# Attention and mixture of experts on one core: loads and splits of the values, and reads of the first slot lists, moved to other turns of the head loop

## The chip, the cores and the metric

The kernel runs on one core of a Trainium2 chip. The metric is device time in microseconds (us) of one execution. Before the change the median of three runs is 532.14 us (531.71 to 534.35).

The engines of the core run side by side, each working through its own instructions strictly in the order in which the program was written: PE (TensorE: matmuls and transposes), DVE (VectorE), ACT (ScalarE), POOL (GpSimd), and SP (SyncE), which here only issues DMA transfers. An instruction that waits holds up everything behind it on its own engine.

## The reference

Causal softmax attention over 4 batches and 12 heads, with 448 positions and 64 numbers a head, then a mixture of 8 experts with one expert per token:

```
scores = q @ k.T / sqrt(64), masked above the diagonal
attn   = softmax(scores);  x = (attn @ v), heads side by side: [1792, 768]
logits = x @ w_gate + modality_bias[modality_id];  e = argmax(logits)
out    = softmax(logits)[e] * (relu(x @ w1[e]) @ w2[e])
```

Everything is float32 in and out. The kernel keeps the accuracy by splitting operands into a high and a low part.

## The kernel before, in words

**The head loop.** `iteration(n)` is called for n = 0 to 47; below it is called turn n. The 48 heads go through it as a pipeline, and one turn does the stages of several heads: scores of head n (`st_scores`, PE line 277), the exponentials of head n-1 (`st_exp`, ACT line 294), the transposes and the split of head n-2 (`st_trans`, PE lines 307 and 309; `st_split`, ACT line 327 and DVE line 328), the product with the values of head n-3 (`st_pv`, PE lines 341 and 348, called PV below), and the sum of its two parts (`st_low`, ACT line 366; `st_out`, DVE line 372, a turn later). Four heads are a group (GH = 4), and three groups are a batch. Group g is heads 4g to 4g+3; its first PV stands in turn 4g+3.

**Combining.** From turn 7 on PE also multiplies one tile of a finished group with the gate weights (`st_comb`, line 401). A turn later it is normalised: tiles 0 and 2 on DVE, tiles 1 and 3 on POOL (lines 419 and 429), for which ACT first copies them out of PSUM (`st_move`, line 411). So in each odd turn POOL begins with a normalisation that needs ACT's copy of what PE did at the end of the turn before.

**Queries and keys.** For each pair of heads m, SP loads `raw` (`load_qk`, line 179). POOL splits it in the odd turn 2m-3 (`split_qk`: line 185, line 186, and two halves of `kz` on line 189). SP then copies parts of the result to the other half of the partitions by four SBUF to SBUF transfers (`stack_qk`, lines 197 and 198), in the even turn 2m-2. The scores of head 2m, in turn 2m, read them.

**Values.** There is a single buffer `vraw` for the values of one group. SP loads it (`load_v`, lines 245 and 246); POOL writes the high part (`split_vh`, line 252) and the low part (`split_vl`, line 257) into `vhl`, of which there are two. The first PV of the group reads both parts. Before the change the values of group g are loaded at the end of turn 4g-2, the high part is made in turn 4g, late, and the low part in turn 4g+1, behind that turn's `split_qk`.

**The list of extra work.** `later(n, f)` puts f into turn n, ahead of `split_qk` and the splits of the values; `before` and `soon` put it at other points of a turn. On POOL these are: setting up constants in turns 4 and 6 to 11 (`shift_slots`, line 553 and 565), scatters of routed tokens into the tables (`scatter`, line 512) in turns 26, 28, 30 and 32 for the first batch and two each in turns 38 and 39 for the second, gathers of tokens (`fetch_x`, line 749), and splits of expert weights in turns 45, 46 and 47 (`w1_chunk`, lines 684 and 685). On SP: the slot lists of the first expert block (`pre_ids`, line 737, four small transfers each, which read the tables) and loads of the first expert's weights (`start_w1`, line 676). The constant n in `after_batch` is 31 for the second batch, to which the numbers 8, 11 and the list W1AT are added. After turn 47 a tail finishes the last heads, and the expert stage follows.

In turn n the order on POOL is: normalisation, list of turn n, `split_qk` (odd n), the group's sums (`st_sums`, turn 4g+1), the splits of the values.

Of the kernel before, what the change touches and what calls it, by code (L numbers as in the profile page):

```python
# [21 lines left out]
def attention_moe(  # L22
# [15 lines left out]
    B, HP, _, _, S = qk.shape  # L38
# [7 lines left out]
    GH = 4  # L46
    NG = H // GH
    NHEAD = B * H
# [97 lines left out]
    def T(shape, dt, tag, bufs):  # L146
        return atp.tile(shape, dt, tag=tag, name=tag, bufs=bufs)
# [44 lines left out]
    def stack_qk(m):  # L192
        st, hl = spl[2 * m]
        u, d = slice(0, 64), slice(64, 128)
        src = hl.bitcast(F32)
        for a, r in enumerate((u, d)):
            nc.sync.dma_start(out=st[u, a].bitcast(F32), in_=src[r, 1:3])
            nc.sync.dma_start(out=st[d, a].bitcast(F32), in_=src[r, 0:3:2])
        for a in range(2):
            spl[2 * m + a] = (st[:, a, 0], st[:, a, 1], hl[:, 1], kz[m % 2][:, a])  # L200

    def clear_kz(j):
        P.memset(kz[j][0:64, 1].bitcast(F32), 0.0)
# [38 lines left out]
    def load_v(gr):  # L242
        b, u = divmod(gr, NG)
        c = slice(u * GH * D, (u + 1) * GH * D)
        nc.sync.dma_start(out=vraw[:, 0:3, :], in_=v[b, 0:384, c].rearrange("(t p) c -> p t c", p=128))
        nc.sync.dma_start(out=vraw[0:64, 3, :], in_=v[b, 384:448, c])
# [3 lines left out]
    def split_vh(gr):  # L250
        t = T([128, NTL, GH, 2, D], F32R, "vhl", 2)
        P.tensor_scalar(out=t[:, :, :, 0], in0=vsrc, scalar1=1.0, scalar2=0.0, op0=ALU.mult, op1=ALU.add)
        vhl[gr] = t
# [115 lines left out]
    def st_out(g):  # L369
        gr, h = divmod(g, GH)  # L370
        j, a = divmod(h, 2)
        V.tensor_tensor(  # L372
            out=ots(gr, j)[a * 64:a * 64 + 64], in0=ov.pop(g)[0:64, :S], in1=ol.pop(g), op=ALU.add
        )
# [10 lines left out]
    def st_rec(gr):  # L385
        V.reciprocal(out=rec[gr], in_=rec[gr])
# [20 lines left out]
    def st_move(gr, i):  # L407
        if i % 2:
            c = cxt[:, (i // 2) * 384:(i // 2) * 384 + GH * XW]
            n = QT[i][1]  # L410
            A.activation(out=c[:n], in_=cx[gr, i][1][:n, :GH * XW], func=AF.Copy)
            cx[gr, i] = P, c
# [21 lines left out]
    def st_norm(gr, i):  # L434
        norm_l(gr, i)
        norm_x(gr, i)

    def x_store(b, i):
        q0, n = QT[i]
        t0 = b * S + q0  # L440
        nc.sync.dma_start(out=xs[t0:t0 + n, :], in_=xrow.pop((b, i))[:n])
# [258 lines left out]
    def reg(apx, engines, lo, hi):  # L700
        return nc.values_load(apx, engines=engines, min_val=lo, max_val=hi, skip_runtime_bounds_check_because=WHY)
# [21 lines left out]
    def places_of(t):  # L723
        return (0, 1) if t < PZ else (t % 2,)

    def fetch_ids(t, off, blk=0):
        d = early.tile([128, NTL, 2, 2], I32, tag="idq", name="idq", bufs=3)
        for i in range(NTL):
            o = d[:, i, blk]
            if t == 0 or PZ <= t < SZ:  # L730
                src = tables[i][bass.ds(off, BLK), :]
            elif t < PZ:
                o = d[:, i]
                src = tables[i][bass.ds(off, 2 * BLK), :].rearrange("(b p) c -> p b c", p=BLK)
            else:
                src = tables[i][bass.ds(off, HB), :].rearrange("(o p) c -> o p c", o=1).to_broadcast([2, HB, 2])
            nc.sync.dma_start(out=o, in_=src)
        idq[t, blk] = d

    def fetch_x(t, rows=NT, blk=None):  # L740
        d = idq.pop((t, blk or 0))
        n = BLK if t < SZ else HB
        for b, u in enumerate(places_of(t)):
            if blk not in (None, b):
                continue
            g = idg[t % 3][b]
            V.tensor_reduce(out=g[:, 0:1], in_=d[:, :, b, 0], axis=AX, op=ALU.min)
            V.tensor_reduce(out=g[:, 1:2].bitcast(F32), in_=d[:, :, b, 1].bitcast(F32), axis=AX, op=ALU.max)
            P.indirect_dma_start(  # L749
                out=xg[u][:n], out_offset=None, in_=xs[0:rows, :],  # L750
                in_offset=bass.IndirectOffsetOnAxis(ap=g[:n, 0:1], axis=0),
                bounds_check=rows - 1, oob_is_err=False,
            )
# [140 lines left out]
    with tc.manual_schedule():  # L894
# [103 lines left out]
        def later(n, f):  # L998
            todo.setdefault(n, []).append(f)

        def before(n, f):
            todo.setdefault((n,), []).append(f)

        def soon(n, f):
            todo.setdefault(-n, []).append(f)

        def run_todo(n):
            for f in todo.pop(n, ()):
                f()

        e0 = []
        W1AT = (7, 9, 14, 14, 15, 15)

        def start_w1(k):
            if k == 0:
                e0.append(reg(sch0[0:1, 0:1], [ET.SP], 0, E - 1))
            load_w(raw1, w1, e0[0], [k])

        def pre_ids(t):
            fetch_ids(0, reg(sch0[0:1, 1 + t:2 + t], [ET.SP], 0, EMPTY), t)  # L1020

        def after_batch(b, n):
            st = route(b)
            if b == B - 1:
                return st
            choose, places, rank, scatter = st
            for j, f in enumerate(choose, 1):
                (later if j % 2 else before)(n + 1 + j // 2, f)
            last = b == B - 2
            soon(n + 4, places)  # L1030
            for j, f in enumerate(rank, 1):
                (later if j % 2 else before)(n + 5 + j // 2, f)
            for i in range(NTL):
                later(n + 7 + (2 * i, i // 2, 0)[b], lambda i=i: scatter([i]))
            if b == 1:
                later(n + 6, first_expert)
                before(n + 7, first_slot)
                for k in range(K1):
                    later(n + W1AT[k], lambda k=k: start_w1(k))
                for j, f in enumerate((first_shift, first_base, first_tri, first_order)):  # L1040
                    later(n + 9 + j, f)
                for t in range(NPRE):
                    later(n + 8 + t, lambda t=t: pre_ids(t))
                    later(n + 11 + 2 * t, lambda t=t: fetch_x(0, 2 * S, t))

        g1b = {}

# [28 lines left out]
        def iteration(n):  # L1076
            if n and n % 2 == 0 and n + 2 < NHEAD:
                stack_qk((n + 2) // 2)
            gr, i = divmod(n - 2 * GH, GH)
            comb = 0 <= gr < B * NG  # L1080
            if 0 <= n - 4 < NHEAD:
                st_out(n - 4)
            if comb:
                st_move(gr, i)
                st_norm(gr, i)
                b, u = divmod(gr, NG)
                if u == NG - 1:
                    later(n + 1, lambda i=i: x_store(b, i))
                    if i == NTL - 1:
                        after_batch(b, n)  # L1090
            run_todo((n,))
            if n in (2, 3):
                st_trans(n - 2)
            if n < NHEAD:
                st_scores(n)
            if n == 0:
                subs.extend(first_split(1))
            if n == 1:
                for f in subs:
                    f()  # L1100
            run_todo(n)
            if n in (1, 3):
                clear_kz(n // 2)
            if n % 2 == 1 and n + 3 < NHEAD:
                split_qk((n + 3) // 2)
            if n % GH == 1 and n > GH:
                st_sums(n // GH - 1, P)
            if n % GH == RECAT and n > GH:
                st_rec(n // GH - 1)
            if n % GH == 1 and n < NHEAD:  # L1110
                split_vl(n // GH)
            if 0 <= n - 1 < NHEAD:
                st_exp(n - 1)
            if n % GH == 0 and n < NHEAD:
                split_vh(n // GH)
            if 0 <= n - 2 < NHEAD:
                if n > 3:
                    st_trans(n - 2)
                run_todo(-n)
                st_split(n - 2)  # L1120
            if 0 <= n - 3 < NHEAD:
                st_pv(n - 3)
                st_low(n - 3)
            gr, i = divmod(n - 2 * GH + 1, GH)
            if 0 <= gr < B * NG:
                st_comb(gr, i)
            if n % 2 == 0 and n + 6 < NHEAD:
                load_qk((n + 6) // 2)
            if n % GH == 2 and n // GH + 1 < B * NG:
                load_v(n // GH + 1)  # L1130

        for n in range(NHEAD):
            iteration(n)
# [47 lines left out]
        n = NHEAD  # L1181
# [238 lines left out]
```

## Time and profile before

| | |
|---|---|
| median of three runs | 532.14 us |
| lowest, highest | 531.71, 534.35 us |
| the profiled execution | 530.7 us, span 529.0 us from the first to the last instruction |
| granted TensorE clock, mean over the span | 0.974 |
| busy share of the span | PE 92%, DVE 60%, POOL 55%, ACT 52% |

The head loop takes about the first 215 us of the span, the expert stage the rest. The profile gives start and duration of each instruction, and for each one before which its engine stood idle, how long and what ended the idle time. Where several waits end together, the one named is the last to come, which need not be the one that mattered. The granted clock is a share: 1.00 is 2.4 GHz, 0.50 is 1.2 GHz.

### The profile page before, as it was taken

The numbers are of one execution on the slowest core, as the hardware profiler recorded it, in microseconds if no ns is written. First come the engines' busy times: TensorE is split into PE (matmuls) and PEld (weight loads), VectorE is DVE, ScalarE is ACT, GpSimd is POOL, SyncE is SP. The second block draws the span as 40 slices with busy tenths as digits, with TensorE's granted clock in tenths as the row PEclk, the third lists the DMA queues.
The fourth block names the chain that finished last, engine by engine and source line by source line (L and its number), as shares of the span: only waits on it lengthen the run. The fifth ranks groups of instructions, "written<-read, shape, count | busy, mean of one in ns | idle before, by whom it ended". The sixth has DMA issues, their size and how long they took to land. (4 is left out here: it accounts for less than half of the span.)

```text
span 529.0 us, 10530 instructions
## 1 busy us (share of the span) xinstructions
PE 486.8 (92%) x3427; PEld 456.9 (86%) x3427; DVE 319.3 (60%) x882; ACT 273.9 (52%) x683; POOL 290.2 (55%) x303
## 2 busy tenths in 40 slices
PE   4598999999988979989899999999999999989981
PEld 4498899999988879878899999999999999978761
DVE  7988888999999979898521114552011120394690
ACT  4498899998878848734321124442111211552830
POOL 7799999889899788973220200742001001194581
PEclk9799999999999979999899999999999999999987
DMA  8687789977977389756369300973101001077100
GB/s 210 176 195 194 198 217 247 277 195 204 241 207 203 114 214 278 240 162 92 90 186 381 93 32 1 295 259 106 62 1 50 31 8 68 20 266 248 25 12 6
DMA packets 44138, 80.77 MB, mean 153 GB/s; under 512 B 15646, under 2 KB 27166, under 8 KB 44064
## 3 DMA queue, kind: packets, MB, share of 16 engines
q1 hardware_dynamic: 41024, 68.89, 46.9%
q0 software_dynamic: 3040, 11.03, 6.3%
q8 instruction: 29, 0.48, 0.4%
q14 instruction: 45, 0.37, 0.3%
HBM read 49.01 MB, written 11.89 MB: 115 GB/s over the span
## 5 line engine op out<-in xcount | busy, mean ns | idle before, releaser
L294 ACT ACTIVATE p<-p,nm 128x448 f32<-128x448 f32 x192 | 94.7, 497 | 9.6 <-DVE nm L284 9.6
L749 POOL DMA_INDIRECT xg<-xs,idg x18 | 20.3, 1128 | 137.2 <-DVEq L1330 73.2
L787 DVE SCALAR_TENSOR_TENSOR htl<-g,hth 128x256 fp32r<-128x256 f32 x40 | 16.8, 423 | 109.5 <-ACT hth L786 109.5
L309 PE MATMUL pt<-ident,p 128*128 128x128 f32 x336 | 70.7, 281 | 0.0
L770 PE MATMUL g<-xh,w1l 128*128 128x256 f32 x240 | 67.9, 283 | 0.0
L769 PE MATMUL g<-xl,w1h 128*128 128x256 f32 x240 | 67.9, 283 | 0.0
L768 PE MATMUL g<-xh,w1h 128*128 128x256 f32 x240 | 67.9, 283 | 0.0
L328 DVE TENSOR_TENSOR pl<-pt,ph 128x1024 fp32r<-128x1024 f32 x48 | 58.4, 1217 | 13.1 <-ACT ph L327 12.9
L327 ACT ACTIVATE ph<-pt 128x1024 fp32r<-128x1024 f32 x48 | 48.9, 1020 | 15.6 <-PE pt L309 15.4
L341 PE MATMUL ot<-ph,vhl 128*128 128x448 f32 x192 | 50.9, 306 | 4.8 <-DVE ut L372 2.3
L189 POOL TENSOR_TENSOR kz<-raw,hl 64x448 fp32r<-64x448 f32 x44 | 51.5, 1170 | 6.4 <-DMA table<-ent,si 4.0
L786 ACT ACTIVATE hth<-g 128x256 fp32r<-128x256 f32 x40 | 15.2, 382 | 65.6 <-PE g L770 64.8
L307 PE MATMUL pt<-ident,p 128*128 128x64 f32 x288 | 49.1, 253 | 0.0
L309 PEld LDWEIGHTS pt<-ident,p 128*128 128x128 f32 x336 | 47.8, 170 | 0.2 <-issue 0.2
L277 PE MATMUL sa<-st 128*128 128x448 f32 x96 | 32.6, 340 | 16.2 <-DVE st L229 6.6
L828 POOL DMA_INDIRECT out_dram<-row,idg x14 | 14.8, 1055 | 57.5 <-ACTq L1314 32.2
L769 PEld LDWEIGHTS g<-xl,w1h 128*128 128x128 f32 x240 | 46.1, 192 | 0.0
L770 PEld LDWEIGHTS g<-xh,w1l 128*128 128x128 f32 x240 | 46.1, 192 | 0.0
L768 PEld LDWEIGHTS g<-xh,w1h 128*128 128x128 f32 x240 | 46.1, 192 | 0.0
L307 PEld LDWEIGHTS pt<-ident,p 128*128 128x128 f32 x288 | 45.0, 197 | 0.4
L341 PEld LDWEIGHTS ot<-ph,vhl 128*128 128x128 f32 x192 | 34.1, 197 | 6.4 <-POOL vhl L257 3.2
L284 DVE CUSTOM_DVE_ANT_0 p<-sa,mask 128x448 f32<-128x448 f32 x96 | 36.2, 413 | 3.3 <-PE sa L277 2.8
(337 smaller groups left out, 1434.1 us busy)
## 6 DMA issues: line engine op xcount, KB each, us to landing
st<-hl SPq DMA_DIRECT2D x88, 224.0 KB
raw<-in_moe_w_dram SPq DMA_DIRECT2D x24, 512.0 KB
raw<-in_qk_dram SPq DMA_DIRECT2D x22, 448.0 KB
raw<-in_moe_w_dram SPq DMA_DIRECT2D x20, 384.0 KB
vraw<-in_v_dram SPq DMA_DIRECT2D x12, 384.0 KB
xs<-row SPq DMA_DIRECT2D x12, 384.0 KB
ut<-in_moe_w_dram SPq DMA_DIRECT2D x6, 384.0 KB
raw<-in_qk_dram SPq DMA_DIRECT2D x8, 224.0 KB
```

The source lines that it names most:

```text
L189: P.tensor_tensor(out=kz[m % 2][r, a], in0=x[r, 1], in1=hl[r, 2].bitcast(F32), op=ALU.subtract)
L277: nc.tensor.matmul(outs[i], lhsT=a[:, q0:q0 + n], rhs=z[:, :w], start=(last == 0), stop=(last == 1))
L284: V.tensor_tensor_reduce(out=z, in0=o, in1=m, scale=-scale, scalar=3.0e38, op0=ALU.add, op1=ALU.min, accum_out=nm[:n, i:i + 1],)
L294: A.activation(out=z, in_=z, func=AF.Exp, bias=nm[:n, i:i + 1], scale=-1.0, accum_out=sums[:n, b, i, h:h + 1],)
L307: nc.tensor.matmul(o, lhsT=a, rhs=ident[:, r0:r1], start=True, stop=True)
L309: nc.tensor.transpose(out=o, in_=a, identity=ident)
L327: A.activation(out=ph, in_=t, func=AF.Copy)
L328: V.tensor_tensor(out=pl, in0=t, in1=ph.bitcast(F32), op=ALU.subtract)
L341: nc.tensor.matmul(o[:, q0:S], lhsT=t[:rows, kt, h].rearrange("p a d -> p (a d)"), rhs=ph[:rows, c0:c1], start=(n == 0), stop=(n == 1),)
L768: nc.tensor.matmul(o, lhsT=ah, rhs=bh, start=first, stop=False)
L769: nc.tensor.matmul(o, lhsT=ah, rhs=bl, start=False, stop=False)
L770: nc.tensor.matmul(o, lhsT=al, rhs=bh, start=False, stop=last)
```

## The change

- The load of the values of group g moves from the end of turn 4g-2 to the top of turn 4g, behind the four stack transfers of that turn. (Group 0 is loaded ahead of the loop, as before.)
- Both splits of the values of group g move to turn 4g+2, one behind the other. Before, they stood in turns 4g and 4g+1.
- The two reads of slot lists move from turns 39 and 40 to turns 41 and 42, and the gathers that use them from turns 42 and 44 to turns 44 and 45.
- The load of the first slice of expert weights moves from turn 38 to turn 39.

```
-        W1AT = (7, 9, 14, 14, 15, 15)
+        W1AT = (8, 9, 14, 14, 15, 15)
...
-                    later(n + 8 + t, lambda t=t: pre_ids(t))
-                    later(n + 11 + 2 * t, lambda t=t: fetch_x(0, 2 * S, t))
+                    later(n + 10 + t, lambda t=t: pre_ids(t))
+                    later(n + 13 + t, lambda t=t: fetch_x(0, 2 * S, t))
...
                 stack_qk((n + 2) // 2)
+            if n and n % GH == 0 and n < NHEAD:
+                load_v(n // GH)
...
-            if n % GH == 1 and n < NHEAD:
+            if n % GH == 2 and n < NHEAD:
+                split_vh(n // GH)
                 split_vl(n // GH)
             if 0 <= n - 1 < NHEAD:
                 st_exp(n - 1)
-            if n % GH == 0 and n < NHEAD:
-                split_vh(n // GH)
...
-            if n % GH == 2 and n // GH + 1 < B * NG:
-                load_v(n // GH + 1)
```

## Rows read from the trace of the kernel before

**Rows 1.** The first part of the profile's page: busy time of each engine, its share of the span, and its instructions.

```profile
PE 486.8 (92%) x3427; PEld 456.9 (86%) x3427; DVE 319.3 (60%) x882; ACT 273.9 (52%) x683; POOL 290.2 (55%) x303
```

**Rows 2.** Waits in the stretch from 12 to 215 us, that is the head loop: who waited for whom, us in total, times, longest. PEld is PE's loading of weights.

```profile
PEld ot L341 <- POOL vhl L257: 3.2, 4, 1.9
PE sa L277 <- DMA st<-hl: 3.1, 1, 3.1
```

**Rows 3.** The timeline of SP in turns 39 and 40: start, duration, instruction. A merged row of several transfers lasts from the first to the last.

```profile
176.89 6.87 SPq L737 DMA_DIRECT2D idq<-table  x4
183.87 0.48 SPq L197 DMA_DIRECT2D st<-hl  x1
```

**Rows 4.** Stretches of the span, from the view by windows: from:to, length, busy time (and count of instructions) of PE, PEld, DVE, ACT and POOL, granted clock, DMA share, GB/s.

```profile
169.24:170.72 1.48, 0.00 (x2) 0.00 (x1) 1.48 (x4) 1.02 (x1) 1.40 (x2) 1.00 0.88 234
185.06:188.17 3.11, 0.00 (x1) 0.03 (x1) 1.78 (x4) 2.10 (x9) 3.03 (x5) 0.95 0.98 217
188.17:195.00 6.83, 6.83 (x34) 6.61 (x34) 5.02 (x13) 1.24 (x2) 6.16 (x6) 0.52 0.74 204
195.00:199.19 4.19, 4.19 (x36) 3.73 (x35) 4.01 (x14) 4.14 (x13) 3.40 (x6) 1.00 0.95 251
252.90:254.79 1.89, 0.00 (x0) 0.00 (x0) 1.28 (x6) 1.89 (x3) 0.33 (x1) 1.00 0.24 4
254.79:259.50 4.71, 4.71 (x18) 4.71 (x19) 4.04 (x10) 0.03 (x1) 1.90 (x2) 0.64 0.58 157
```

**Rows 5.** The timeline of POOL in turns 4 to 6 (group 1): start, duration, instruction.

```profile
33.06 1.06 POOL L252 TENSOR_SCALAR vhl<-vraw 128x1024 fp32r<-128x1024 f32 x1
39.00 2.35 POOL L257 TENSOR_TENSOR vhl<-vraw,vhl 128x1024 fp32r<-128x1024 f32 x1
41.32 0.46 POOL L553 TENSOR_SCALAR by_shift<-tcol 128x1 f32<-128x1 f32 x2
41.84 0.34 POOL L553 TENSOR_SCALAR by_shift<-by_shift 128x1 f32<-128x1 f32 x2
```

**Rows 6.** The timeline of PE: the first PV of groups 1 and 2, with PE's idle time before it.

```profile
41.40 0.56 PE L341 MATMUL ot<-ph,vhl 128*128 128x448 f32 x2 [1.67 <-POOL vhl L257]
58.08 0.56 PE L341 MATMUL ot<-ph,vhl 128*128 128x448 f32 x2 [0.64 <-POOL vhl L257]
```

**Rows 7.** The timeline of POOL in turns 24 to 31 (groups 6 and 7).

```profile
109.82 1.04 POOL L252 TENSOR_SCALAR vhl<-vraw 128x1024 fp32r<-128x1024 f32 x1
112.75 0.24 POOL L419 TENSOR_TENSOR ltp<-cxt,rec 128x32 f32<-128x32 f32 x1 [1.89 <-ACT cxt L411]
...
118.44 2.39 POOL L257 TENSOR_TENSOR vhl<-vraw,vhl 128x1024 fp32r<-128x1024 f32 x1
...
127.84 1.03 POOL L512 DMA_INDIRECT table<-ent,si  x1 [0.28 <-POOL kz L189]
128.95 1.04 POOL L252 TENSOR_SCALAR vhl<-vraw 128x1024 fp32r<-128x1024 f32 x1
...
134.59 1.17 POOL L189 TENSOR_TENSOR kz<-raw,hl 64x448 fp32r<-64x448 f32 x1 [0.54 <-DMA table<-ent,si]
...
136.13 2.39 POOL L257 TENSOR_TENSOR vhl<-vraw,vhl 128x1024 fp32r<-128x1024 f32 x1
138.66 1.01 POOL L512 DMA_INDIRECT table<-ent,si  x1
139.70 0.25 POOL L419 TENSOR_TENSOR ltp<-cxt,rec 128x32 f32<-128x32 f32 x1
```

**Rows 8.** The timeline of PE: the first PV of groups 7, 10 and 11.

```profile
138.57 0.56 PE L341 MATMUL ot<-ph,vhl 128*128 128x448 f32 x2
...
197.37 0.55 PE L341 MATMUL ot<-ph,vhl 128*128 128x448 f32 x2
...
214.09 0.54 PE L341 MATMUL ot<-ph,vhl 128*128 128x448 f32 x2
```

**Rows 9.** The timeline of POOL in turns 36 to 46 (groups 9 to 11).

```profile
162.07 1.04 POOL L252 TENSOR_SCALAR vhl<-vraw 128x1024 fp32r<-128x1024 f32 x1
163.66 0.24 POOL L419 TENSOR_TENSOR ltp<-cxt,rec 128x32 f32<-128x32 f32 x1 [0.54 <-DMA st<-hl]
...
191.26 2.36 POOL L257 TENSOR_TENSOR vhl<-vraw,vhl 128x1024 fp32r<-128x1024 f32 x1
...
195.85 0.23 POOL L419 TENSOR_TENSOR ltp<-cxt,rec 128x32 f32<-128x32 f32 x1 [0.71 <-DMA xs<-row]
...
200.95 1.17 POOL L189 TENSOR_TENSOR kz<-raw,hl 64x448 fp32r<-64x448 f32 x1 [1.04 <-DMA xg<-xs,idg]
...
210.00 2.40 POOL L257 TENSOR_TENSOR vhl<-vraw,vhl 128x1024 fp32r<-128x1024 f32 x1
212.37 1.05 POOL L684 TENSOR_SCALAR w1h<-raw 128x1024 fp32r<-128x1024 f32 x1
213.50 2.39 POOL L685 TENSOR_TENSOR w1l<-raw,w1h 128x1024 fp32r<-128x1024 f32 x1
```

**Rows 10.** Two lines of the program by themselves: engine, operation, count, shortest, median and longest duration in ns, first and last start in us.

```profile
L257 POOL TENSOR_TENSOR vhl<-vraw,vhl x12: 2344/2382/2404, 19.5 to 210.0; 128x1024 fp32r<-128x1024 f32 x12
L695 POOL TENSOR_TENSOR w1l<-raw,w1h x3: 3399/3402/3406, 336.6 to 501.7; 128x1024 fp32r<-128x1024 f32 x3
```

**Rows 11.** The timeline of POOL: the high part of group 5, the one that waited for its load inside the loop.

```profile
95.11 1.04 POOL L252 TENSOR_SCALAR vhl<-vraw 128x1024 fp32r<-128x1024 f32 x1 [0.74 <-DMA vraw<-in_v_dram]
```

## The prediction

> **What bounds the kernel now.** I read the busy shares first, then PE's waits, then the timelines of SP, POOL and PE around each wait. PE is busy 92% of the span, POOL 55% [rows 1]; that average hides that in the head loop PE and POOL run neck and neck. PE's waits there that touch the change have two causes [rows 2]: the values' split on POOL (3.2 us as seen by weight loads, four times) and one stack transfer (3.1 us). The second is the one that the change seems made for. SP holds the first slot-list read from 176.89 to 183.87, and the stack transfer of the next pair stands behind it [rows 3]; PE is idle from 185.06 to 188.17 and then works 6.83 us at a granted clock of 0.52, near the lower level (1.2 GHz), on a turn; the next turn, at 1.00, takes 4.19 [rows 4]. So that stall costs 3.11 + (6.83 - 4.19 = 2.64) = 5.75 us.
>
> The first cause looks small but shows a balance without slack. The first PV of groups 1 and 2 waits 1.67 and 0.64 us for the low part [rows 6]; that of group 7 starts at 138.57, just behind the low part's end at 136.13 + 2.39 = 138.52 [rows 7, 8]. Where POOL does get ahead it can't use it: at 112.75 it has been idle 1.89 us, waiting for ACT's copy of PE's last combining, which opens its odd turn [rows 7]. POOL's chain is thus: PE ends turn 4g, POOL normalises, splits queries and keys, splits values, PE starts the PV in turn 4g+3.
>
> **The change, part by part.** The moved splits cost 1.04 and about 2.38 us each [rows 7, 10]. Before, the high part stands ahead of the normalisation, where POOL would often idle anyway; afterwards both stand behind the split of queries and keys and behind turn 4g+2's list. What is added ahead of a first PV is therefore the high part (1.04), wherever POOL waited for ACT, and whatever the list puts into turn 4g+2.
>
> *Groups 1 to 3.* POOL is continuously busy from group 1's high part on, so moving that costs nothing there. But turn 6's four constants (0.46 + 0.34 = 0.8, about 0.9 with gaps) now come ahead of the low part instead of behind it [rows 5]: group 1's PV waits 2.5 instead of 1.67. In group 2 PE is 0.9 later, so POOL waits for ACT and the high part no longer fills that wait; with half as many constants in turn 10 (0.4 by the same rows) the added chain is 1.04 + 0.4 less what 0.9 already covers, 0.5. Group 3 gives a little back. I take 1.2; the bounds are 0.9 (group 1 alone) and 1.5.
>
> *Groups 6 and 7, turns 25 to 31.* I follow POOL from 112.75, where it waits for PE in either version, to group 7's low part. Added: group 6's high part (1.04, at 109.82 it lay before the wait); the scatter of turn 30, from 138.66 to the next instruction at 139.70 with its gap about 1.2; and group 7's high part. The last lay at 128.95 between the scatter of 127.84 and a half of kz which at 134.59 had waited for just that scatter, 6.75 us after its issue [rows 7]. Out of there it doesn't shorten that stretch, since the scatter sets its end, and it comes again behind it: 1.04. Sum 3.3 us, all of it on PE since the PV of group 7 had no slack. PE would stand 0.8 of it in turn 27 and the rest, 2.5 and its old 0.3, in turn 31. If the scatter lands sooner the third term goes: lower bound 2.2.
>
> *Groups 9 to 11, turns 37 to 47.* I follow POOL from 163.66, where it again waited (0.54), to group 11's low part, which ended at 210.00 + 2.40 = 212.40, 1.69 ahead of its PV at 214.09 [rows 8, 9]. Added: group 9's high part (1.04, at 162.07) and the expert weights of turn 46, which now stand ahead of group 11's splits (212.37 to 213.50 + 2.39 = 215.89: 3.52). Taken away: two waits of 0.71 and 1.04, of which the second was for the gather that leaves turn 42. The two gathers and four scatters stay in this stretch. So the low part ends 1.04 + 3.52 - 1.75 = 2.81 later against turn 37, and the PV 2.81 - 1.69 = 1.1 later. This holds although the 5.75 us of the stack transfer go: group 10's low part ended at 191.26 + 2.36 = 193.62, and its PV at 197.37 would, without the stall, be due at 191.6. POOL is 2.0 late there already and gets 1.04 later. The gain turns into waits of turns 43 and 47 for POOL, some 3 to 4 us each.
>
> *SP's parts.* With the slot lists read in turns 41 and 42 the scatters have landed, and SP issues the stack transfers when POOL has their data: the wait of rows 3 goes, costed above. Its four reads still take SP's time, behind turn 40's transfers, where nothing is due for a turn. The value loads wait for less than before, since their buffer is free two turns earlier; they are issued behind four stack transfers about two turns ahead of their use, as far ahead as before, when one split waited for its load for 0.74 us [rows 11]; I take 0, bounds 0 and +0.7. The first weight slice, a turn later, is used in turn 45, and the gathers' tokens only in the tail: 0; if a gather were late there, the nearest row is the 1.04 of rows 9.
>
> *The clock.* PE idle for 1.48 kept it at 1.00; 1.89 was followed by a stretch at 0.64 and 3.11 by one at 0.52 [rows 4]. New waits of 2.5 (turn 7), 2.8 (turn 31) and 3 to 4 (turns 43 and 47) lie nearest to the rows that lowered it. A lowered clock costs 2.64 by rows 4 where PE sets the pace, and nothing where POOL is the later one anyway, as in turn 43. The bounds are 0 and 3 times 2.64 = 7.9. I take one, behind turn 31, where PE goes on alone: 2.6.
>
> Sum: 1.2 + 3.3 + 1.1 + 2.6 = 8.2 us slower. The profiled execution took 530.7 (span 529.0), so 538.9; the median of the runs is 1.4 above it, and 532.1 + 8.2 = 540.3.
>
> **One rule weighed.** The low part took 2344 to 2404 ns in all twelve groups, beside whatever DVE did; an instruction of the same shape on line 695, in the expert stage, took 3402 [rows 10]. The Trainium skill ("SBUF — State Buffer", section "SBUF: two separate sides") says that DVE and GpSimd share a port pair as an exclusive lock: a DVE instruction with two SBUF inputs blocks a GpSimd one outright. If moved splits came to lie beside such instructions, they would take 1.02 more each (3402 - 2382); that is the last rival.
>
> **The rivals.**
> 1. *Faster: the stack transfer decides (0.12).* Its place is turn 42. If POOL's added work finds cover, the 5.75 go and only the lateness that POOL has in group 10 today (2.0) comes in their place: 532.1 - 3.7 = 528.4. For it speaks that this is the longest single wait for a transfer in the loop [rows 2]; against it, that POOL has no cover where the waits of rows 6 and 7 show it. It decides if group 10's low part ends before 191.6 plus the shift that turns 7 to 31 have given.
> 2. *No change (0.14).* Groups 6 and 7 cost little, because scatters land early and the PV's wait is met by PE's own delays, and the clock stays up: 1.2 + 1.1 = 2.3, so 534.4. This is also what comes out if slot lists or stack transfers still hold SP and the change does less than it says.
> 3. *Much slower: the clock falls behind three of the waits (0.12).* 1.2 + 3.3 + 1.1 + 7.9 = 13.5: 545.6.
> 4. *By the port rule (0.03).* Eight splits without slack, 1.02 each, on top of the forecast: 548.5.
>
> **How the numbers follow.** The forecast has 0.59: POOL's order is written out and its durations hardly vary, so the sign of the sum is firmer than its size. With the clock term between 0 and two falls (5.3) and the other bounds, its own range is 535 to 543. Within 0.5% of 532.1 is 529.5 to 534.8, about what a measurement of this kernel can tell from no change. Faster 0.12 (rival 1), same 0.14 (rival 2), slower 0.59 + 0.12 + 0.03 = 0.74. The range reaches down past rival 2 to 531 and up to rival 3 at 546; left out are rival 1 (0.12), rival 4 (0.03) and little of the rest.
>
> **What would show it.** Right: PE's first PVs of groups 1, 6, 7, 10 and 11 wait for the low part, most in turns 31, 43 and 47; POOL idles for ACT's copy ahead of turn 4g+1's normalisation in the quiet groups; the stack transfer of turn 40 goes out within 3 us of POOL's split and no wait of PE names it; a stretch of lowered clock lies behind turn 31 and none at the scores of head 42. Wrong: first PVs that don't wait in turns 27 to 31, which would say that POOL had cover that I don't see; a low clock at other places; or weight splits of turn 46 that let group 11's splits pass in time.

## The result and the profile after

The change makes the kernel slower. On the chip of the first comparison the median went from 531.92 us (4 runs) to 539.14 us (4 runs, 535.98 to 541.54), a ratio of 1.0137 [1.0097, 1.0178], or +7.2 us. On another chip it was 534.28 to 538.90: 1.0097 [1.0059, 1.0134], or +4.6. The forecast was +8.2 and 540.3.

The profiled execution took 539.93 us, span 538.2, mean granted clock 0.966. Busy time first, from the profile's page, to be held against [rows 1]:

```profile
PE 490.6 (91%) x3427; PEld 458.9 (85%) x3427; DVE 315.8 (59%) x882; ACT 273.8 (51%) x683; POOL 289.4 (54%) x303
```

Every engine runs the same number of instructions as before, and only PE, with its loading of weights, is busier (486.8 to 490.6 us): the same work, part of it at a lowered clock. So the loss is waiting and clock, not work. The waits in the head loop, 12 to 225 us (who waited for whom, total us, times, longest), against [rows 2]:

```profile
PEld ot L341 <- POOL vhl L257: 12.9, 7, 3.1
PE ot L341 <- POOL vhl L257: 11.7, 7, 2.9
...
POOL kz L189 <- DMA table<-ent,si: 3.4, 2, 2.2
```

The stack transfer is gone from PE's waits. The wait for the low part went from 3.2 to 12.9 us as weight loads see it. SP's timeline shows why the first went (start, duration, instruction); before, the slot lists held this transfer until 183.87 [rows 3]:

```profile
185.99 0.49 SPq L197 DMA_DIRECT2D st<-hl  x1
...
194.11 2.50 SPq L737 DMA_DIRECT2D idq<-table  x4
```

It now goes out as soon as POOL's split ends, and the slot lists follow 8 us later. The price stands on PE's timeline: the first PV of groups 1, 2, 6, 7, 9, 10 and 11, with PE's idle time before it, against [rows 6, 8]:

```profile
40.85 0.67 PE L341 MATMUL ot<-ph,vhl 128*128 128x448 f32 x2 [1.88 <-POOL vhl L257]
...
59.54 0.56 PE L341 MATMUL ot<-ph,vhl 128*128 128x448 f32 x2 [1.21 <-POOL vhl L257]
...
125.50 0.56 PE L341 MATMUL ot<-ph,vhl 128*128 128x448 f32 x2 [1.09 <-POOL vhl L257]
...
143.90 0.90 PE L341 MATMUL ot<-ph,vhl 128*128 128x448 f32 x2 [2.39 <-POOL vhl L257]
...
181.84 0.56 PE L341 MATMUL ot<-ph,vhl 128*128 128x448 f32 x2 [0.47 <-POOL vhl L257]
...
201.08 0.55 PE L341 MATMUL ot<-ph,vhl 128*128 128x448 f32 x2 [2.92 <-POOL vhl L257]
...
222.16 0.90 PE L341 MATMUL ot<-ph,vhl 128*128 128x448 f32 x2 [1.75 <-POOL vhl L257]
```

POOL's timeline in turns 28 to 31 and in turn 46 shows what stands ahead of the low part, against [rows 7, 9]:

```profile
131.00 1.03 POOL L512 DMA_INDIRECT table<-ent,si  x1 [0.28 <-POOL kz L189]
...
137.35 1.17 POOL L189 TENSOR_TENSOR kz<-raw,hl 64x448 fp32r<-64x448 f32 x1 [1.17 <-DMA table<-ent,si]
...
139.32 1.01 POOL L512 DMA_INDIRECT table<-ent,si  x1 [0.51 <-issue]
140.36 1.06 POOL L252 TENSOR_SCALAR vhl<-vraw 128x1024 fp32r<-128x1024 f32 x1
141.50 2.35 POOL L257 TENSOR_TENSOR vhl<-vraw,vhl 128x1024 fp32r<-128x1024 f32 x1
...
215.10 1.06 POOL L684 TENSOR_SCALAR w1h<-raw 128x1024 fp32r<-128x1024 f32 x1
216.24 2.42 POOL L685 TENSOR_TENSOR w1l<-raw,w1h 128x1024 fp32r<-128x1024 f32 x1
218.61 1.06 POOL L252 TENSOR_SCALAR vhl<-vraw 128x1024 fp32r<-128x1024 f32 x1
219.75 2.35 POOL L257 TENSOR_TENSOR vhl<-vraw,vhl 128x1024 fp32r<-128x1024 f32 x1
```

The scatter, the high part and the weight split of 1.06 + 2.42 all stand ahead of the low part now, and the PV starts at once when it ends (143.85 and 143.90; 222.10 and 222.16).

Last the windows (from:to, length, busy time of PE, PEld, DVE, ACT, POOL, granted clock, DMA share, GB/s): PE behind the waits of turns 7, 31, 43 and 47, and, third, the scores of head 42, against [rows 4]:

```profile
40.85:43.88 3.03, 3.03 (x12) 2.24 (x12) 1.57 (x2) 1.04 (x3) 2.85 (x5) 0.55 0.39 105
...
143.90:147.17 3.27, 3.27 (x13) 2.45 (x13) 0.47 (x1) 1.05 (x3) 3.19 (x5) 0.50 0.23 59
...
191.72:195.54 3.82, 3.82 (x33) 3.75 (x34) 3.82 (x15) 3.21 (x11) 3.67 (x5) 1.00 0.88 244
...
201.08:205.00 3.92, 3.92 (x16) 3.06 (x16) 2.59 (x7) 2.12 (x8) 3.84 (x5) 0.56 0.70 164
222.16:227.36 5.20, 5.20 (x31) 4.38 (x32) 1.92 (x5) 2.51 (x9) 5.12 (x5) 0.68 0.45 171
```

The turn of head 42, 6.83 us at 0.52 before, takes 3.82 at 1.00. In return four other stretches run wholly or in part at the lower of the two levels (0.50 to 0.68).

### The profile page after: what moved, and what is told of

Read it like the earlier page. It is cut to its first block, busy times and chain, and to the rows that moved or that the text cites. A ratio compares the mean times of both kernels' runs of the same rounds, so it can differ in the third digit from the quotient of the medians.

```text
span 538.2 us, 10519 instructions
## 1 busy us (share of the span) xinstructions
PE 490.6 (91%) x3427; PEld 458.9 (85%) x3427; DVE 315.8 (59%) x882; ACT 273.8 (51%) x683; POOL 289.4 (54%) x303
## 5 line engine op out<-in xcount | busy, mean ns | idle before, releaser
L341 PE MATMUL ot<-ph,vhl 128*128 128x448 f32 x192 | 52.0, 312 | 14.6 <-POOL vhl L257 11.7
L341 PEld LDWEIGHTS ot<-ph,vhl 128*128 128x128 f32 x192 | 35.0, 202 | 17.1 <-POOL vhl L257 12.9
L366 ACT ACTIVATE hol<-ot 64x448 f32<-64x448 f32 x48 | 26.0, 542 | 26.1 <-PE ot L341 24.5
```

What stands on the lines that cost most here:

```text
L341: nc.tensor.matmul(o[:, q0:S], lhsT=t[:rows, kt, h].rearrange("p a d -> p (a d)"), rhs=ph[:rows, c0:c1], start=(n == 0), stop=(n == 1),)
L366: A.activation(out=t, in_=ov[g][64:128, :S], func=AF.Copy)
```

## The experiments

All were timed against the kernel before on the same chip. On the three chips used its medians were 535.28, 534.28 and 534.63, so ratios are compared, not times. One per cent is 5.3 us.

**The two kernels again.** First what a single profile is worth.

> The kernel before, unchanged, timed against itself on the chip of the next three and with a profile from that chip: ratio 1.000 (0.997 to 1.003). Theory: the chip sets several us of the span, so this profile, and not the first one, is the one that the profiles of the other three are to be held against; it would end 2 to 5 us later than 529.0 with the same waits. Rival: its span is 529 again, and then the profiles of the kernels with the lists alone and with the splits first (530.7 and 535.1) stand against their timed ratios (0.993 and 1.001).

> The changed kernel, unchanged, on the same chip as the next two: ratio 1.0137 again, within 1.010 to 1.018, about 539. Its profile should again show lowered clock behind turns 7, 31, 43 and 47 and first products waiting there for the low part of the values; a stretch that is not there a second time was chance and not the change.

Measured: 0.9998 [0.9977, 1.0019], and 1.0097 as given above. The theory on the profile of before held: its span was 534.5. Of the 5.5 us, 1.9 come in turns 34 to 36, behind a wait of PE for DVE, 0.8 in the stall that the change removes, 1.2 in turns 43 to 45 and 1.1 in the expert stage. The stall (windows of its profile, the wait and the turn behind it):

```profile
187.23:192.06 4.83, 0.01 (x1) 0.04 (x1) 1.82 (x4) 2.14 (x9) 4.66 (x6) 0.77 0.68 146
192.06:198.04 5.98, 5.98 (x34) 5.82 (x34) 4.29 (x13) 1.17 (x2) 5.06 (x6) 0.61 0.70 170
```

With the next turn at 4.22 us the stall cost 4.83 + (5.98 - 4.22) = 6.6 us there, where [rows 4] gave 5.75. In the second profile of the changed kernel the first PV of turn 31 waits 1.99, of turn 43 2.51 and of turn 47 1.75, each with a lowered clock behind it; behind turn 31 it was lowered for less long than in the first profile (the window from that PV to the scores of head 33):

```profile
142.46:149.66 7.20, 7.20 (x45) 6.33 (x46) 3.88 (x14) 3.66 (x11) 6.26 (x8) 0.76 0.77 202
```

Turn 7 was different: its wait was there, 2.27 us, but the clock stayed at 1.00 (PE's timeline, and the window behind it):

```profile
41.41 0.56 PE L341 MATMUL ot<-ph,vhl 128*128 128x448 f32 x2 [2.27 <-POOL vhl L257]
```
```profile
41.41:44.41 3.00, 3.00 (x21) 2.54 (x22) 1.84 (x5) 1.71 (x6) 2.82 (x5) 1.00 0.31 85
```

So behind turn 7 the lowered clock is chance; the wait was there both times.

**The two halves of the change apart.** The kernel before with the list parts alone:

```
-        W1AT = (7, 9, 14, 14, 15, 15)
+        W1AT = (8, 9, 14, 14, 15, 15)
...
-                    later(n + 8 + t, lambda t=t: pre_ids(t))
-                    later(n + 11 + 2 * t, lambda t=t: fetch_x(0, 2 * S, t))
+                    later(n + 10 + t, lambda t=t: pre_ids(t))
+                    later(n + 13 + t, lambda t=t: fetch_x(0, 2 * S, t))
```

> The kernel before, with the slot-list reads, gathers and the first weight load moved as in the change; loads and splits of the values stay where they were. Theory (POOL's chain sets the head loop; the stack transfer that waits behind the list reads costs 5.75 us, of which the lateness of 2.0 us that POOL has in group 10 comes back): 532 - 3.7 = about 528.3; no idle time of PE at the scores of head 42, a wait of about 2 us at the first PV of group 10, no low clock near there. Rival 1 (the stack transfer alone decides): 526.2, and no wait at that PV. Rival 2 (slot lists don't matter, something else takes the place of the stall at once): 532.

> The kernel before with the moved list parts alone, a second time, since with group 0's splits added the ratio was 0.9967 where 0.990 was expected. Theory: the gain of the lists is 0.993 (0.990 to 0.996) and group 0's splits add nothing, since the gain is waited away in turn 35. Rival: the first value was high by chance and it is 0.996 to 0.999.

Measured: 0.9931 [0.9903, 0.996], the second time 0.9968 [0.9939, 0.9997]. The lists alone are a gain, of 1.7 to 3.7 us; no change, the second rival of the first run, falls, and so does the first (526.2, no wait at group 10's PV). The second value lies in the range of its own rival; which of the two sizes is right stays open, since the intervals overlap. The gain is smaller than the stall: group 10's first PV now waits, 3.33 us in this profile and 2.75 in that of the second run, which ended 4.3 us earlier. Ahead of it half of kz in turn 39 waits for the second batch's scatters to land, 5.11 and 2.85 us, where the first profile of the kernel before has 2.59 (POOL, then PE, of the first run):

```profile
186.15 1.15 POOL L189 TENSOR_TENSOR kz<-raw,hl 64x448 fp32r<-64x448 f32 x1 [5.11 <-DMA table<-ent,si]
```
```profile
196.48 0.56 PE L341 MATMUL ot<-ph,vhl 128*128 128x448 f32 x2 [3.33 <-POOL vhl L257]
```

This is POOL's lateness in group 10 of the prediction (2.0 us), and here it is 3.3.

The changed kernel with the list parts as before, that is the same lines undone:

> The changed kernel with the slot-list reads, gathers and the first weight load back where they were; loads and splits of the values stay moved. Theory: the chain on POOL gets the gather of turn 42 and its wait back (1.1 + 1.0 us) ahead of group 10's and 11's splits, and the stack transfer of head 42 waits for the scatters again, this time with POOL later: 1 to 4 us slower than the changed kernel, 540 to 543. Rival (the list part is what made the changed kernel slow): near the kernel before, 532. In either case the head loop up to turn 36 should look like that of the changed kernel, with a first PV of group 7 that waits about 2.4 us.

Measured: 1.0151 [1.011, 1.0192]. The value parts alone cost 8 us, so the whole loss is theirs. That this is more than the full change costs fits the theory, but the difference lies within the intervals. In its profile PE waits for the stack transfers again, 3.89 us at the scores of head 42 and 2.91 at those of head 44.

**What in the value parts costs: the list that stands ahead.** The changed kernel with both splits ahead of the list in every turn 4g+2:

```
+            if n % GH == 2 and n < NHEAD:
+                split_vh(n // GH)
+                split_vl(n // GH)
             run_todo(n)
...
-            if n % GH == 2 and n < NHEAD:
-                split_vh(n // GH)
-                split_vl(n // GH)
```

> The changed kernel with both splits of the values put ahead of the list of extra work in turn 4g+2, so that constants, scatters and the weight split of turn 46 no longer stand ahead of them. What is left against the kernel with the list reads alone is the loss of cover of the high part. Theory: the terms of the list go (0.9 in group 1, 0.4 in group 2, 1.2 in turn 30, 3.5 in turn 46), the cover terms stay (1.04 in groups 6, 7, 9 and 10): 531 to 534, a wait of about 1.5 at group 7's first PV, about 3 at group 10's, none at group 11's. Rival (the splits of both parts in one turn are late whatever stands ahead, or the later load is the cause): 537 to 540, as the changed kernel.

Measured: 1.0011 [0.9982, 1.0039]. The theory's range held, and the rival's (537 to 540 of 532) is out. The list ahead of the splits is worth 0.9 to 1.3% against the two runs of the changed kernel, 4.6 to 6.7 us. What remains against the lists alone, 0.4 to 0.8% or 2.3 to 4.3 us, the prediction puts down to the cover that the high part lost; no kernel here has that by itself. The later load of the values is not the cause: neither in this profile nor in the two of the changed kernel does POOL wait for it. The profile also shows a wait that no step had: the first PV of group 8, in turn 35.

```profile
139.18 0.56 PE L341 MATMUL ot<-ph,vhl 128*128 128x448 f32 x2 [1.71 <-POOL vhl L257]
...
159.60 0.56 PE L341 MATMUL ot<-ph,vhl 128*128 128x448 f32 x2 [2.33 <-POOL vhl L257]
```

With PE less late out of turn 31, POOL is behind for one more group.

Then two parts of the list by themselves. First only turn 46, where group 11's splits go ahead of the weight split:

```
+            if n == 46:
+                split_vh(11)
+                split_vl(11)
             run_todo(n)
...
-            if n % GH == 2 and n < NHEAD:
+            if n % GH == 2 and n < NHEAD and n != 46:
```

> The changed kernel with group 11's two splits ahead of turn 46's list, so that the split of expert weights (1.06 + 2.42, 3.5 us with gaps) stands behind them again. Theory: that split is what makes the first product of turn 47 wait 1.75 us and lowers the clock behind it (about 1.5 us more); without it the product starts at its own due time and the clock stays up: 3 us off, 535.5 to 536.5 where the changed kernel takes 539, ratio 1.003 to 1.008 where that stood at 1.0137 and 1.0097. Rival: the weights are then 3.5 us late for the tail and the expert stage takes the 3 us back: 1.009 to 1.014.

Measured: 1.0027 [1.0003, 1.0051], just under the theory's range, which its interval reaches; the rival falls. In its profile the first PV of turn 47 waits for nothing, and the turn behind it runs at 1.00:

```profile
222.61:226.34 3.73, 3.73 (x36) 3.31 (x34) 3.41 (x14) 3.53 (x11) 3.65 (x4) 1.00 0.23 46
```

That is 5.20 - 3.73 = 1.47 us of clock, beside the 1.75 of the wait: 3.2 us. From the PV of head 47 to the end it takes 303.5 us, the changed kernel 303.0 and 303.4: the weights, split later, are not missed in the tail. Against the changed kernel the ratios are 0.7 to 1.1% lower, 3.7 to 5.9 us. This profile does not show where the rest of that comes from: with 539.44 us its execution was the second longest of twelve.

Second only the first batch's scatters, moved behind the splits:

```
-                later(n + 7 + (2 * i, i // 2, 0)[b], lambda i=i: scatter([i]))
+                (later if b else soon)(n + 7 + (2 * i, i // 2, 0)[b], lambda i=i: scatter([i]))
```

> The changed kernel with the first batch's four scatters (turns 26, 28, 30 and 32) behind the splits of the values on POOL instead of ahead of them. Theory: the scatter of turn 30 is 1.2 us of the 2.0 to 2.4 us for which the first product of turn 31 waits; it goes to about 1 us, the clock behind it stays up (1.5 us), and turn 27 waits no more: scores of head 33 come 2.5 to 4 us earlier against the changed kernel, of which 1 to 2 are lost again in turn 35; ratio 1.006 to 1.009. Rival: the half of kz that waits for a scatter to land meets it in turns 29 and 31 instead, POOL gains nothing, and the first product of turn 35 (group 8) waits over 2 us: 1.010 to 1.014.

Measured: 1.011 [1.0067, 1.0152]. The theory falls, the rival holds (with the wait for the scatter mostly in turn 33). Turns 27 and 31 do get their microseconds: scores of head 33 start at 146.56, where the changed kernel has 152.50 and 149.66. They are lost again in turn 33, where half of kz waits for a scatter, and in turn 35 (POOL, then PE):

```profile
148.35 1.01 POOL L512 DMA_INDIRECT table<-ent,si  x1 [0.50 <-DVE ut L372]
...
155.84 1.16 POOL L189 TENSOR_TENSOR kz<-raw,hl 64x448 fp32r<-64x448 f32 x1 [2.36 <-DMA table<-ent,si]
```
```profile
41.34 0.56 PE L341 MATMUL ot<-ph,vhl 128*128 128x448 f32 x2 [2.50 <-POOL vhl L257]
...
140.85 0.56 PE L341 MATMUL ot<-ph,vhl 128*128 128x448 f32 x2 [1.61 <-POOL vhl L257]
...
160.90 0.90 PE L341 MATMUL ot<-ph,vhl 128*128 128x448 f32 x2 [3.17 <-POOL vhl L257]
```

The scatter of 148.35 and its kz lie 7.5 us apart, those of 131.00 and 137.35 in the changed kernel 6.35, and before the change 127.84 and 134.59 [rows 7] 6.75. In these three the scatter sets when the next split of queries and keys ends, ahead of the splits of the values or behind them.

**What the lowered clock costs.** The changed kernel with the ten transposes of `st_trans` done twice, to the same result, in turns 7, 31, 43 and 47, so that PE works where it would wait:

```
+        for _ in range(2 if g + 2 in (7, 31, 43, 47) else 1):
             tr(pa[:, 320:448], p[3][:, 0:128], 0, 128)
...
```

> The changed kernel in which PE makes the ten transposes of a turn twice in turns 7, 31, 43 and 47, the same result again, about 1.2 us of added work each, in the stretch in which it then waits for the values' low part. The idle time gets shorter by that much, and the waits end when they did. Theory (the lowered clock behind turn 31 costs 2 to 3 us, behind turn 7 and 47 about 1 each, behind turn 43 nothing because POOL sets the pace): granted clock stays at 1.00 in turns 8, 32 and 48; 535 to 537 instead of 539. Rival (the low clock costs nothing, POOL and DVE set the pace behind it): 539; or, if the waits end later for the added work, 540 to 542.

> The changed kernel with the transposes done twice in turns 7, 31, 43 and 47, a second time. Theory: PE busy through those waits keeps the clock up and the waits for the low part stay as far as PE would have been early; the ratio is 1.0033 again (1.000 to 1.007), and no stretch of lowered clock stands behind turns 31 and 47. Rival: the first result was the chip's: 1.009 to 1.014 as for the changed kernel.

Measured: 1.0033 [1.0003, 1.0062] and 1.0018 [0.9989, 1.0047]. More work on PE makes the kernel faster by 0.6 to 1.2%, 3 to 6 us, where the first expectation had 2 to 4. The mean granted clock goes with it: over the runs its median is 0.976 to 0.977, in the two sets of the changed kernel 0.967 and 0.969. The windows behind the waits of turns 31 (two of them) and 47, of the second run:

```profile
143.44:145.27 1.83, 1.83 (x12) 1.40 (x13) 0.93 (x1) 0.53 (x2) 1.75 (x4) 1.00 0.65 257
145.27:149.14 3.87, 3.87 (x35) 3.80 (x34) 3.46 (x13) 3.17 (x11) 3.52 (x4) 1.00 0.75 170
223.51:227.27 3.76, 3.76 (x31) 3.33 (x32) 2.22 (x5) 3.28 (x10) 3.68 (x4) 1.00 0.59 222
```

From the first PV of turn 31 to scores of head 33 it takes 5.70 us; in the two profiles of the changed kernel 152.50 - 143.90 = 8.60 and 149.66 - 142.46 = 7.20. So the clock behind turn 31 cost 2.9 us in the one and 1.5 in the other, behind turn 47 1.4 to 1.5.

In these places the theory holds, but the two profiles do not show the gain of the whole. In both PE then waits 2.01 us for the low part of group 8 in turn 35 and 2.6 for a stack transfer at the scores of head 42, each with a lowered clock behind it in the second (0.51 and 0.61), and the first PV behind turn 47 starts at 227.48 and 227.27, where the changed kernel has 227.36 and 226.02. Both profiled executions (542.96 and 539.37 us) were longer than the medians of their runs (537.69 and 536.94). Which of the places the other runs keep, no trace here tells.

**Can both be beaten?** Of the value parts one looked like a gain: scores of head 4 start 1.0 to 1.5 us earlier after the change. The lists alone with group 0's splits in turn 2:

```
+            if n == 2:
+                split_vh(0)
+                split_vl(0)
-            if n % GH == 1 and n < NHEAD:
+            if n % GH == 1 and GH < n < NHEAD:
...
-            if n % GH == 0 and n < NHEAD:
+            if n and n % GH == 0 and n < NHEAD:
```

> The kernel before with the moved list parts, and of the value parts only group 0's two splits in turn 2; groups 1 to 11 as before. Theory: the gain at the start (scores of turn 4 about 1.5 us earlier) is a matter of group 0's splits alone, which hold up a small DVE instruction in turn 1 where they stand before; it adds to the 3.7 us of the lists: ratio 0.990 (0.987 to 0.993), about 527 of 532. Rival: POOL's chain sets the first product of group 1, so that the 1.5 us are waited away in turn 7: 0.993 as with the lists alone.

Measured: 0.9967 [0.994, 0.9993]. The 1.5 us are there at the start (scores of head 4 at 25.36, before 26.84), and at scores of head 20 they are still there (90.25 and 91.62). But from scores of head 36 on the kernel is level with the lists alone (158.98 and 159.13). The rival is right that the gain is waited away, but not where. About 1 us went in this profile at scores of head 22, in a wait for a transfer; in the next kernel's profile that wait is missing, the gain lasts to turn 34, and scores of head 36 still start at 159.43. What takes it in both is turn 35 (PE's timeline).

```profile
157.14 0.56 PE L341 MATMUL ot<-ph,vhl 128*128 128x448 f32 x2 [2.11 <-POOL vhl L257]
```

The same, with the second batch's scatters behind the splits of turns 38 and 39 (`soon` instead of `later` for them):

> As the last one, and the second batch's scatters of turns 38 and 39 stand behind that turn's splits on POOL instead of ahead of them. Theory: with the lists alone half of kz waited 5.1 us in turn 39 for those scatters to land, which made group 10's low part 2.8 us later than before, and its first product waited 3.3 us with a lowered clock behind; with the scatters behind the splits the wait goes and the stack transfer for head 42 is in time: 3 to 5 us less than the last one, ratio 0.983 (0.979 to 0.987). Rival: the scatters then land later and the slot lists of turn 41 hold SP instead, so that scores of head 42 or 44 wait for their stack transfer: 0.988 to 0.995.

Measured: 0.9968 [0.9942, 0.9993]. The theory falls: kz still waits, in two turns instead of one, and group 10's PV is still late (POOL, then PE):

```profile
180.73 1.16 POOL L189 TENSOR_TENSOR kz<-raw,hl 64x448 fp32r<-64x448 f32 x1 [1.94 <-DMA table<-ent,si]
...
190.62 1.15 POOL L189 TENSOR_TENSOR kz<-raw,hl 64x448 fp32r<-64x448 f32 x1 [0.99 <-DMA table<-ent,si]
```
```profile
194.54 0.56 PE L341 MATMUL ot<-ph,vhl 128*128 128x448 f32 x2 [2.77 <-POOL vhl L257]
```

So the lists alone, 0.3 to 0.7% under the kernel before, are the best version found here, and neither addition made it better. The wait of kz for a scatter is in the program as it was built. In the kernel before, between the two halves of [rows 7], POOL has an instruction of line 189 that does nothing but wait for a semaphore; the profile names the scatter as what ended it (instruction, count, durations in ns, start in us):

```profile
L189 POOLq EVENT_SEMAPHORE  x1: 17/17/17, 134.5 to 134.5; - x1
```

Why it was put there, no run tells.

## Why the prediction was right, and where its terms were off

The direction and the mechanism were right: POOL's added work ahead of the first PVs. The size, 8.2 us against 7.2 on one chip and 4.6 on the other, is in part luck, since the sum came out of terms some of which were wrong in opposite directions. Its own range was also added up loosely: the bounds that the prediction gives (0.9, 2.2, 1.1 and 0; 1.5, 3.3, 1.1, 0.7 and 5.3) make 536.3 to 544.0, not 535 to 543. The table sets the sum against two pairs of profiles, by the starts of scores (S) and first PVs: each entry is how much longer the stretch takes after the change, in us. The first pair is the first profile of each kernel, the second the two of the same chip.

| stretch | forecast | first pair | second pair |
|---|---|---|---|
| start to S4 | 0 | -1.5 | -1.0 |
| S4 to S25 (groups 1 to 3) | +1.2 | +3.1 | +1.6 |
| S25 to S33 (groups 6 and 7, clock) | +5.9 | +6.6 | +4.5 |
| S33 to S37 | 0 | -2.1 | -3.6 |
| S37 to first PV of turn 47 (groups 9 to 11) | +1.1 | +1.9 | +0.8 |
| the turn's stretch behind it, to the next PV | 0 | +1.5 | +1.5 |
| to the end | 0 | -0.3 | -1.0 |
| sum | +8.2 | +9.2 | +2.8 |

- **The stack transfer's stall goes and is turned into POOL's waits**: as forecast. From S41 to S43 the kernel before takes 14.06 and 14.91 us, the changed one 8.02 and 8.05, so 6.0 to 6.9 go (forecast 5.75). From S43 to S44 4.2 come back in both pairs, in the first as the wait of 2.92 for the low part and 1.3 more, most of it at the lowered clock behind that wait, and from S44 to the first PV of turn 47 another 3.0 to 3.3, of which 1.75 are its wait (forecast: waits of 3 to 4 in each).
- **The list ahead of the splits** (constants, scatters, weights) was the larger part of the loss, shown by the kernels with the splits first and with the weights behind. The weights' 3.5 us were in the sum, but only as part of a balance that 1.69 of slack and 1.75 of shorter waits brought down to 1.1; back behind the splits they gave 3.2 us at that place, since a lowered clock came with them.
- **Groups 6 and 7**: waits of 1.09 in turn 27 and 2.39 in turn 31, 1.99 in the second profile (forecast 0.8 and 2.8). Their parts can't be taken singly: without the scatter ahead the same time is waited in turn 35. The prediction let POOL's shortage end with group 7. It reaches group 8, and in the changed kernel, where PE comes later out of turn 31, that was hidden.
- **The step that failed: that what turns 25 to 31 lose stays lost.** From S33 to S37 2.1 to 3.6 us come back. Before, PE waits there for DVE's routing of the first batch (L487; 1.24 us in the first profile of before, and in the second 1.25 with a lowered clock behind it); in both profiles after the change PE does not wait there, so that work is done by the time PE comes to it. The row is of PE's timeline in the second profile of before:

```profile
157.63 0.18 PE L487 MATMUL x<-oh,upper 128*128 128x32 bf16 x1 [1.25 <-DVE oh L477]
```

- **The clock**: one fall of 2.6 behind turn 31 was taken, and it cost 2.9 in the first pair and 1.5 in the second, which is most of what parts the two pairs in that row. Turn 47 also lowered it, with 1.5, which the sum left out. The fall behind turn 43 was put at nothing, since POOL would be the later one anyway; yet the turn is longer by 1.3 beside its wait, and POOL was idle for 0.92 ahead of its normalisation in turn 45, waiting for ACT's copy, so that the argument held only in part. Rival 3 put 2.64 on each fall; behind turn 7 one cost 1.2 (3.03 to scores of head 8, and 1.82 in the second profile), which is part of the first pair's +3.1, and behind turn 47 1.5.
- **The start** was put at nothing and gave 1.0 to 1.5 back (below).
- Rival 1 (faster) is what the lists do alone. It lost because the value parts cost 8 us. Rival 4 is out: the low part took 2342 to 2397 ns in all twelve groups.

The two kernels' profiles differ by 9.2 us or by 2.8, though the timed medians differ by 7.2 and 4.6. One profile of each would have been a poor witness for the size. For the places it was a good one: the waits stood in the same turns in both.

## What to carry to other kernels

Before work is moved on an engine that runs neck and neck with the bottleneck, look at what its old place was: if the engine idled there anyway, the work was free, and in a place behind a chain it costs its full length, and everything that the new order puts ahead of it as well. Take the parts of such a change one by one; here one half gained 0.3 to 0.7% and the other lost 1.5%. And a wait removed or added on such a pair of engines travels: follow it to the next point where the other engine would have waited in any case, since there it is given back.

## What the runs showed of the hardware that was not expected

**DVE held by POOL.** In turn 1 of the kernel before, a DVE instruction on 128 x 8 elements lasts 2.31 us, the next one of the same shape 0.17. DVE, then POOL at the same time, in the second profile of before:

```profile
19.60 2.31 DVE L972 TENSOR_SCALAR ebase<-evals 128x8 f32<-128x8 f32 x1
21.94 0.17 DVE L973 TENSOR_SCALAR ebneg<-ebase 128x8 f32<-128x8 f32 x1
```
```profile
19.52 2.36 POOL L257 TENSOR_TENSOR vhl<-vraw,vhl 128x1024 fp32r<-128x1024 f32 x1
```

It ends at 21.91, POOL's low part of group 0 at 21.88. After the change the high part stands there, and the same instruction lasts as long as that:

```profile
19.40 1.01 DVE L972 TENSOR_SCALAR ebase<-evals 128x8 f32<-128x8 f32 x1
20.45 0.17 DVE L973 TENSOR_SCALAR ebneg<-ebase 128x8 f32<-128x8 f32 x1
```
```profile
19.33 1.06 POOL L252 TENSOR_SCALAR vhl<-vraw 128x1024 fp32r<-128x1024 f32 x1
```

Each time the two instructions end within 0.03 us of each other. The masks and maxima of scores (line 284), for which PE waits in turn 3, stand behind it on DVE; scores of head 3 started 1.0 to 1.5 us earlier after the change. The Trainium skill ("SBUF — State Buffer", section "SBUF: two separate sides") says that DVE and GpSimd share a port pair as a lock, and whichever starts first has it for its whole instruction; of DVE it counts instructions with two SBUF inputs or in a mode that uses two ports. These rows agree, with POOL first by 0.08 and 0.07 us; this DVE instruction has one input, and its mode no trace shows. The prediction had weighed only the other side of it, DVE holding POOL up.

**The length of PE's wait alone does not say whether the clock falls.** Behind waits of 1.75 us (turn 47) and 1.88 (turn 7) it was lowered, in the changed kernel; behind 2.27 in the second run of the same kernel and behind 2.50 with the scatters moved, both in turn 7, it stayed at 1.00:

```profile
41.34:44.30 2.96, 2.96 (x20) 2.51 (x21) 1.56 (x5) 1.66 (x6) 2.78 (x5) 1.00 0.33 93
```

The prediction had gone by the waits of 1.48 and 1.89 in [rows 4]; these runs are not divided by the length of the wait. What else decides, they leave open.
